# Squares of u on POOL and ACT only, sums of e on POOL only, with another order table

## The chip, the core and the metric

The kernel runs on one core of one Trainium2 chip. The metric is the device time of one execution in microseconds; lower is better. Before the change three runs gave 202.01, 202.43 and 203.88 us, median 202.43 us.

## What is computed

The reference does two steps. The first is attention without softmax over 8 batches of 8 heads, 576 tokens and 64 channels: per head `kv = k^T v`, `o = q kv`, and `o` is divided by its root mean square over the 64 channels and multiplied by `g_norm`. The second step takes the 4608 tokens of 512 channels through a feed-forward layer:

```python
h = x @ w_in                       # 512 -> 1024
e = np.exp(h - h_max)
solu = h * e / (sum(e) + 1e-9)
ln = (solu - mu) / np.sqrt(var + 1e-6) * g_ln
out = ln @ w_out                   # 1024 -> 512
```

The kernel never forms `solu`. It forms `u = h * exp(h)`, and for the layer norm it needs per token the sum of u, the sum of the squares of u, and the sum of e (only for the 1e-6 term). The mean is taken out of `w_out` beforehand, so the matmul `out = u @ w_out` needs only a factor per token at the end.

## The kernel before, in words

The 4608 tokens are cut into 9 chunks (`c` = 0 to 8) of 512. Chunks 0 to 7 hold the first 512 tokens of a batch, chunk 8 the 64 that are left of each. Each chunk passes through these pieces, whose names the texts below use:

- loads by the POOL queue: `k.c.g`, `v.c.g`, `q.c.g`, `q_last.c` (lines 298 and 308), and once `w_in`, `w_out`;
- `qT_mm`, `qT`: q is transposed on TensorE and copied out (chunks 0 to 3), or transposed by a DMA from the SP queue (chunks 4 to 8);
- `kv_mm`, `kv`: k^T v on TensorE, copied to `kvd` by DVE or ACT (line 210);
- `o_mm`, `sq`, `s_mm`, `ln`, `ex`, `x`: q kv on TensorE, squares on ACT, their mean over a head by a matmul, its -1/2 power in two ACT instructions, and the product on DVE;
- `h.c.f.part`: for each of 8 blocks f of 128 hidden channels, a matmul of x by w_in into a PSUM bank (line 464), in two halves for chunks 0 to 2;
- `exp.c.f` on ACT (line 471) and `u.c.f` on DVE (line 475): `e` in f32, `u` in bf16;
- `usq.c.f`: the square of u, bf16, 128x512 (line 479, by the helper `square` in lines 212 to 216; on ACT it is an activation, on POOL and DVE a tensor_tensor with u as both inputs);
- `es.c.n`: the sum of two neighbouring e, f32 to bf16 (lines 481 to 483), a tensor_tensor with two inputs in SBUF;
- `sums.c`: matmuls that sum u, usq and es over the hidden channels (line 508), so it needs all 8 u, 8 usq and 4 es of the chunk; then `turn.c`, `stats.c` (DVE) and `rstd.c` (ACT);
- `out.c.m.part` (line 562), `ob.c.m` (scaling by rstd on DVE or ACT) and `store.c.m`.

Nothing is scheduled at run time by hand: the pieces are issued in the order of the string `ORDER` (lines 20 to 88) by `Plan.emit`, and every engine carries out its own instructions in that order. A suffix such as `:dve` or `:act` names the engine; without one, it is the first in the piece's list of engines, as in

```python
add(("usq", c, f), "pool|act|dve", lambda e, c=c, f=f: u_sq(e, c, f), [("u", c, f)], [("u", c), ("usq", c)])
add(("es", c, n), "pool|dve", lambda e, c=c, n=n: e_sum(e, c, n), [("exp", c, f - 1), ("exp", c, f)], [("e", c, n), ("es", c)])
```

A buffer pool bounds how far pieces may run ahead: 3 buffers each for k, v, q and qT, 4 for e (each holds two blocks), 2 each for u, usq and es, 4 for ob. An `exp` that takes a fifth e buffer waits for the `es` and the two `u` that read the first one. The string `HOME` says in which kind of PSUM bank (h, out, o, s, misc; 8 banks in all) a piece's result lies where it is not the usual one.

Before the change the 72 squares are 32 on POOL, 29 on DVE and 11 on ACT; the 36 sums of e are 24 on POOL and 12 on DVE. POOL also issues the 36 loads.

Of the kernel before, what the change touches and what calls it, by code (L numbers as in the profile page):

```python
# [20 lines left out]
warm k.0.0 q.0.0 v.0.0 v.0.1 k.0.1 q.0.1 w_in.1 ident turn_g warm.0 qT_mm.0.0 warm.3 kv_mm.0.0 kv.0.0.2:act warm.1  # L21
kv.0.0.1:act qT.0.0 kv.0.0.0 o_mm.0.0 warm.4 warm.5 g_mean sq.0.0.1 sq.0.0.0 s_mm.0.0.0 s_mm.0.0.1 w_in.0 q.1.0 v.1.0
k.1.0 ex.0.0.1 q.1.1 kv_mm.0.1 kv.0.1.1 x.0.0.1 qT_mm.0.1 qT.0.1 kv.0.1.0:act k.1.1 kv.0.1.2:act warm.2 warm.6
ex.0.0.0 o_mm.0.1 sq.0.1.1 sq.0.1.0 x.0.0.0 s_mm.0.1.1 h.0.6.0 ex.0.1.1 s_mm.0.1.0 ex.0.1.0 x.0.1.1 h.0.4.0 h.0.7.0
x.0.1.0 h.0.3.0 table h.0.7.1 h.0.6.1 h.0.2.0 exp.0.7 h.0.4.1 qT_mm.1.0 h.0.3.1 v.1.1 exp.0.4 exp.0.6 h.0.2.1 u.0.7
qT.1.0 w_out.0 exp.0.3 h.0.1.0 w_out.1 h.0.0.0 u.0.6 exp.0.2 h.0.1.1 exp.0.1 u.0.3 kv_mm.1.0 kv.1.0.2:act kv.1.0.1:act
h.0.0.1 u.0.2 q.2.0 kv.1.0.0 u.0.4 h.0.5.0 usq.0.3:dve u.0.1 o_mm.1.0 exp.0.0 qT_mm.1.1 h.0.5.1 sq.1.0.1 qT.1.1
s_mm.1.0.1 k.2.0 usq.0.7 v.2.0 es.0.1 es.0.3 usq.0.6 sq.1.0.0 kv_mm.1.1 q.3.0 ln.1.0.1 u.0.0 usq.0.2:dve s_mm.1.0.0
exp.0.5 kv.1.1.2 kv.1.1.0 kv.1.1.1 o_mm.1.1 u.0.5 ex.1.0.1 ln.1.0.0 sq.1.1.0 w_mean.0 s_mm.1.1.0 ex.1.0.0 es.0.0
sq.1.1.1 ln.1.1.0 s_mm.1.1.1 ln.1.1.1 x.1.0.1 es.0.2:dve usq.0.0 usq.0.5 x.1.0.0 usq.0.4:dve ex.1.1.0 ex.1.1.1 x.1.1.0  # L30
usq.0.1 h.1.3.0 h.1.1.0 x.1.1.1 w_mean.1 sums.0 w_center.2 turn.0 h.1.5.0 w_center.0 v.4.0 h.1.1.1 qT_mm.2.0 h.1.2.0
exp.1.1 w_center.1 h.1.0.0 k.4.0 u.1.1 stats.0 h.1.3.1 h.1.0.1 qT.2.0:act k.3.0 w_center.3 w_center.5 v.3.0 out.0.0.0
qT_mm.2.1 exp.1.3 out.0.0.1 w_center.4 h.1.5.1 rstd.0 exp.1.0 qT.2.1:act w_center.6 w_center.7 u.1.3 u.1.0 h.1.2.1
out.0.0.2 exp.1.5 exp.1.2 kv_mm.2.0 h.1.4.0 out.0.0.3 kv.2.1.1:act kv.2.0.0 kv.2.0.2:act u.1.2 kv.2.1.0:act v.6.0
h.1.4.1 kv.2.0.1:act kv.2.1.2:act o_mm.2.0 qT_mm.3.0 ob.0.0 qT.3.0 es.1.0 q.4.0 sq.2.0.0 out.0.1.0 usq.1.3 sq.2.0.1
s_mm.2.0.0 out.0.1.1 qT.4 out.0.2.0 ln.2.0.0 exp.1.4 out.0.1.2 s_mm.2.0.1 out.0.1.3 ex.2.0.0 out.0.2.1 ln.2.0.1 u.1.5
u.1.4 ob.0.1:act ex.2.0.1 qT_mm.3.1 h.1.6.0 o_mm.2.1 sq.2.1.1 x.2.0.1 out.0.2.2 h.1.6.1 s_mm.2.1.1 out.0.3.0 qT.3.1
sq.2.1.0 exp.1.6 x.2.0.0 u.1.6 ln.2.1.1 usq.1.5 usq.1.1 out.0.2.3 s_mm.2.1.0 out.0.3.1 h.1.7.0 es.1.1 ln.2.1.0
ex.2.1.1 out.0.3.2 ex.2.1.0 x.2.1.1 ob.0.2 kv_mm.4.0 h.2.0.0 h.1.7.1 x.2.1.0 kv.4.1.0 usq.1.4:dve kv.4.1.1 out.0.3.3
exp.1.7 h.2.6.0 kv.4.0.0:act kv.4.0.1:act ob.0.3:act kv.4.0.2:act kv.4.1.2:act h.2.4.0 h.2.7.0 h.2.4.1 es.1.2:dve  # L40
usq.1.0 h.2.0.1 h.2.6.1 h.2.7.1 kv_mm.3.0 usq.1.6 store.0.0 store.0.1 u.1.7 usq.1.2:dve store.0.3 es.1.3 exp.2.4
exp.2.0 exp.2.7 u.2.4 h.2.2.0 h.2.5.0 h.2.3.0 h.2.5.1 usq.2.4 u.2.0 kv.3.0.2 store.0.2 kv.3.1.2:act exp.2.6 u.2.7
usq.1.7:dve kv.3.0.1:act h.2.1.0 kv.3.1.1 u.2.6 q_last.7 h.2.2.1 kv.3.0.0 exp.2.5 h.2.1.1 kv.3.1.0 exp.2.2 o_mm.3.0
exp.2.1 usq.2.0 es.2.3 sq.3.0.1 u.2.5 sums.1 s_mm.3.0.1 u.2.2 sq.3.0.0 turn.1 h.2.3.1 out.1.0.0 es.2.0 ln.3.0.1 u.2.1
exp.2.3 stats.1 usq.2.1:dve o_mm.3.1 out.1.0.1 u.2.3 s_mm.3.0.0 out.1.2.0 usq.2.2:dve rstd.1 sq.3.1.0 sq.3.1.1 ob.1.0
ex.3.0.1 x.3.0.1 usq.2.7 s_mm.3.1.1 out.1.2.1 ln.3.0.0 out.1.1.0 s_mm.3.1.0 ex.3.0.0 ln.3.1.1 q_last.2 ln.3.1.0
ex.3.1.0 es.2.2:dve x.3.0.0 out.1.1.1 ob.1.2 out.1.3.0 o_mm.4.1 ex.3.1.1 x.3.1.0 sq.4.1.0 out.1.3.1 x.3.1.1 sq.4.1.1
s_mm.4.1.0 usq.2.3:dve h.3.0.1 ln.4.1.0 ob.1.3 ex.4.1.0 ob.1.1 x.4.1.0 exp.3.0 h.3.7.1 v.5.0 h.3.3.1 k.5.0 usq.2.5
es.2.1 exp.3.7 usq.2.6:dve u.3.7 u.3.0 exp.3.3 s_mm.4.1.1 o_mm.4.0 sums.2 ln.4.1.1 sq.4.0.1 turn.2 ex.4.1.1 stats.2
h.3.2.1 store.1.0 sq.4.0.0 h.3.1.1 s_mm.4.0.1 exp.3.2 x.4.1.1 u.3.3 u.3.2 rstd.2 h.3.6.1 s_mm.4.0.0 ln.4.0.1 q_last.4  # L50
out.2.3.0 ex.4.0.1 q.5.0 k.6.0 h.3.5.1 x.4.0.1 qT.5 store.1.2 ln.4.0.0 exp.3.6 out.2.3.1 exp.3.5 exp.3.1 ex.4.0.0
u.3.6 kv_mm.5.0 kv_mm.6.0 ob.2.3 kv.5.0.0:act kv.5.1.2:act kv.5.1.0:act usq.3.3 x.4.0.0 u.3.5 kv.6.1.1 kv.5.1.1:act
es.3.1 h.3.4.1 kv.6.1.2:act store.1.1 k.7.0 kv.5.0.1:act out.2.1.0 exp.3.4 kv.5.0.2 o_mm.5.0 out.2.1.1 kv.6.0.2 u.3.4
sq.5.0.0 kv.6.1.0:act kv.6.0.1:act u.3.1 v.7.0 es.3.3 q_last.5 q_last.3 store.1.3 s_mm.5.0.0 ln.5.0.0 sq.5.0.1 ob.2.1
out.2.2.0 q.6.0 q_last.6 usq.3.5:dve o_mm.5.1 kv.6.0.0 out.2.2.1 ex.5.0.0 sq.5.1.1 sq.5.1.0 ob.2.2:act es.3.0
s_mm.5.0.1 store.2.3 out.2.0.0 qT.6 s_mm.5.1.1 usq.3.6 ln.5.1.1 out.2.0.1 x.5.0.0 ob.2.0 usq.3.7 ln.5.0.1 h.4.5.1
kv_mm.7.0 h.4.1.1 ex.5.1.1 ex.5.0.1 x.5.1.1 es.3.2 kv.7.1.2 usq.3.1:dve exp.4.5 usq.3.4:dve u.4.5 kv.7.1.0:act h.4.6.1
h.4.4.1 s_mm.5.1.0 usq.3.2 exp.4.1 exp.4.6 exp.4.4 ln.5.1.0 x.5.0.1 u.4.6 kv.7.0.2 usq.3.0 usq.4.5 kv.7.1.1 u.4.1
h.4.3.1 ex.5.1.0 x.5.1.0 exp.4.3 h.4.0.1 sums.3 h.4.2.1 h.4.7.1 usq.4.1:dve u.4.4 kv.7.0.0:act store.2.2 exp.4.0 u.4.0
turn.3 exp.4.2 u.4.3 stats.3 u.4.2 exp.4.7 h.5.0.1 out.3.1.0 o_mm.6.0 out.3.1.1 out.3.3.0 rstd.3 kv.7.0.1 u.4.7  # L60
usq.4.2:dve sq.6.0.0 s_mm.6.0.0 ob.3.1:act out.3.3.1 store.2.0 out.3.0.0 ln.6.0.0 store.2.1 ob.3.3:act sq.6.0.1
out.3.2.0 es.4.0 usq.4.3:dve usq.4.0:act ex.6.0.0 s_mm.6.0.1 out.3.0.1 q_last.1 store.3.1 es.4.1 out.3.2.1 usq.4.7
x.6.0.0 usq.4.6:dve usq.4.4:dve es.4.2 ob.3.0:act ln.6.0.1 es.4.3 exp.5.0 q.7.0 ex.6.0.1 u.5.0 qT.7 o_mm.6.1 h.5.1.1
sums.4 h.5.3.1 ob.3.2 sq.6.1.0 sq.6.1.1 exp.5.1 exp.5.3 turn.4 s_mm.6.1.0 h.5.2.1 x.6.0.1 h.5.6.1 ln.6.1.0 store.3.3
exp.5.2 ex.6.1.0 exp.5.6 u.5.1 stats.4 u.5.3 h.5.5.1 out.4.1.0 s_mm.6.1.1 ln.6.1.1 u.5.2 u.5.6 exp.5.5 x.6.1.0
out.4.1.1 u.5.5 h.5.4.1 out.4.3.0 rstd.4 h.5.7.1 ex.6.1.1 x.6.1.1 ob.4.1 exp.5.7 exp.5.4 out.4.0.0 u.5.7 es.5.1
usq.5.0 q_last.0 o_mm.7.0 u.5.4 out.4.3.1 store.3.2 ob.4.3 out.4.0.1 sq.7.0.1 store.3.0 usq.5.5:dve sq.7.0.0
s_mm.7.0.1 s_mm.7.0.0 es.5.3:dve ob.4.0 usq.5.1 usq.5.7:act es.5.2 es.5.0:dve ln.7.0.0 out.4.2.0 h.6.7.1 ex.7.0.0
h.6.2.1 usq.5.3:dve x.7.0.0 out.4.2.1 ln.7.0.1 usq.5.6:dve h.6.4.1 qT.8 h.6.1.1 store.4.1 exp.6.7 usq.5.4:act usq.5.2
exp.6.2 ob.4.2 ex.7.0.1 u.6.2 exp.6.1 u.6.7 store.4.0 x.7.0.1 sums.5 o_mm.7.1 turn.5 exp.6.4 sq.7.1.0 sq.7.1.1 h.6.6.1  # L70
stats.5 h.6.0.1 s_mm.7.1.0 u.6.1 u.6.4 exp.6.6 store.4.2 u.6.6 s_mm.7.1.1 h.6.5.1 exp.6.0 h.6.3.1 out.5.1.0 u.6.0
usq.6.4:dve ln.7.1.0 ln.7.1.1 exp.6.5 exp.6.3 out.5.2.0 u.6.5 es.6.3 store.4.3 out.5.0.0 out.5.1.1 usq.6.0 usq.6.2:act
ex.7.1.0 ex.7.1.1 u.6.3 x.7.1.0 out.5.2.1 x.7.1.1 rstd.5 o_mm.8.0 out.5.0.1 out.5.3.0 sq.8.0.1 sq.8.0.0 ob.5.2
s_mm.8.0.0 out.5.3.1 ob.5.1:act store.5.1 ln.8.0.0 es.6.1 s_mm.8.0.1 ob.5.0 usq.6.5:dve h.7.6.1 es.6.2:dve store.5.0
ob.5.3 store.5.3 usq.6.7:dve h.7.7.1 es.6.0:dve h.7.3.1 usq.6.1 ln.8.0.1 usq.6.3 ex.8.0.0 exp.7.7 exp.7.3 exp.7.6
x.8.0.0 usq.6.6:dve u.7.7 es.7.3:dve h.7.2.1 store.5.2 exp.7.2 out.6.3.0 u.7.3 sums.6 h.7.5.1 out.6.3.1 turn.6
ex.8.0.1 x.8.0.1 exp.7.5 out.6.2.0 u.7.2 stats.6 u.7.5 u.7.6 o_mm.8.1 out.6.2.1 sq.8.1.0 sq.8.1.1 rstd.6 s_mm.8.1.0
ob.6.3:act out.6.0.0 s_mm.8.1.1 ln.8.1.0 usq.7.2 ln.8.1.1 ex.8.1.1 out.6.0.1 h.7.1.1 exp.7.1 ob.6.2 ex.8.1.0 u.7.1
# [78 lines left out]
def kernel(  # L157
# [35 lines left out]
    add = plan.add  # L193
# [36 lines left out]
    q_last = big.tile([128, NP, B, D], BF16, name="q_last")  # L230
# [254 lines left out]
    for c in range(NC):  # L485
        for f in range(NF):
# [9 lines left out]
            if f % 2:  # L496
                n = f // 2
                add(("es", c, n), "pool|dve", lambda e, c=c, n=n: e_sum(e, c, n), [("exp", c, f - 1), ("exp", c, f)], [("e", c, n), ("es", c)])
# [135 lines left out]
```

## Time and profile before

| | |
|---|---|
| median of three runs | 202.43 us (202.01 to 203.88) |
| profiled execution, its own time | 204.0 us |
| its span, first to last instruction | 202.2 us |
| mean granted TensorE clock | 0.975 |
| PE busy | 178.0 us, 88% |
| DVE busy | 142.1 us, 70% |
| ACT busy | 141.2 us, 70% |
| POOL busy | 96.5 us, 48% |
| DMA | 29.71 MB, mean 147 GB/s |

Engines are PE (TensorE matmul), DVE (VectorE), ACT (ScalarE), POOL (GpSimd) and SP (a queue that issues DMAs). The profile page gives busy time per engine, forty equal slices of the span with the busy share of each in tenths, the groups of instructions with their mean duration, and the chain of work that ended last. The trace gives the same by window, by tile and as a timeline; there a row has start, duration, engine, line and shape, and in brackets the idle time of the engine in front of it with what ended it. Consecutive matmuls overlap at their ends, so the distance from start to start is the cost of one in a run, and the same holds to a lesser degree for ACT and DVE.

### The profile page before, as it was taken

The page shows a single profiled execution, that of the slowest core. Times are in us where ns is not written, and L with a number is a line of the kernel's source. Part 1 is how long each engine was busy: PE and PEld are TensorE (multiplying, and loading weights), DVE is VectorE, ACT ScalarE, POOL GpSimd, SP SyncE. Part 2 cuts the span into 40 slices and gives each one's busy share as a digit, 9 for nine tenths or more (in the row PEclk, how much of TensorE's full clock was granted, in tenths as well). Part 3 has the DMA queues.
Part 4 walks back from the last instruction along what each step waited for, and adds up shares of the span by engine and source line. Part 5 has one row for each costly group of instructions (what it writes and reads, how often), then busy time and mean ns, then how long its engine had stood idle before and what let it go on. Part 6 is the DMA issues. An engine that isn't in the chain of part 4 may idle for free.

```text
span 202.2 us, 5289 instructions
## 1 busy us (share of the span) xinstructions
PE 178.0 (88%) x2174; PEld 87.0 (43%) x2199; DVE 142.1 (70%) x266; ACT 141.2 (70%) x250; POOL 96.5 (48%) x106
## 2 busy tenths in 40 slices
PE   7677955999999488999869999999999999989991
PEld 2342532564444143355224544544544454445540
DVE  1145699688489988877847973869986782799440
ACT  2068873567989496998947769969796749885232
POOL 7942894805934994029961383164065031506000
PEclk9999996699999999999978999999999999999999
DMA  3999999999988769999997327787510622230265
GB/s 54 194 204 207 206 385 229 207 208 208 209 135 186 143 65 188 225 212 172 212 156 181 85 16 119 143 170 156 130 28 3 149 63 70 59 79 3 69 148 203
DMA packets 35544, 29.71 MB, mean 147 GB/s; under 512 B 16440, under 2 KB 30016, under 8 KB 35520
## 3 DMA queue, kind: packets, MB, share of 16 engines
q0 software_dynamic: 19104, 17.30, 52.1%
q1 hardware_dynamic: 16128, 11.54, 24.5%
q10 hardware_dynamic: 288, 0.52, 0.7%
q8 instruction: 17, 0.28, 0.6%
q14 instruction: 7, 0.06, 0.1%
HBM read 32.51 MB, written 9.44 MB: 207 GB/s over the span
## 4 chain that ended last, share of the span: by engine, by line
PE 53%; DVE 20%; ACT 14%; issue 5%; DMA 5%; POOL 1%; ACTq 0%; DVEq 0%; POOLq 0%
PE out_ps L562 21%; PE h_ps L464 19%; DVE u_sb L475 6%; PE misc_ps L508 5%; DVE usq_sb L216 5%; ACT e_sb L471 4%; DMA v_sb<-in_v_dram 3%; PE s_ps L407 3%; ACT osq_sb L214 3%; ACT rst_sb L415 3%; ACT lss_sb L411 2%; PE o_ps L395 2%; DVE x_sb L427 2%; DVE kvd L210 2%; DMA out_dram<-ob_sb 2%
## 5 line engine op out<-in xcount | busy, mean ns | idle before, releaser
L562 PE MATMUL out_ps<-w_out_sb,u_sb 128*128 128x512 bf16 x279 | 70.4, 384 | 2.3 <-DVE u_sb L475 1.4
L464 PE MATMUL h_ps<-x_sb,w_in_sb 128*128 128x512 bf16 x274 | 69.2, 384 | 2.0 <-issue 0.7
L471 ACT ACTIVATE e_sb<-h_ps,zero_t 128x512 f32<-128x512 f32 x72 | 47.6, 686 | 14.3 <-PE h_ps L464 13.1
L475 DVE TENSOR_TENSOR u_sb<-h_ps,e_sb 128x512 bf16<-128x512 f32 x72 | 47.6, 683 | 10.8 <-ACT e_sb L471 10.2
L216 POOL TENSOR_TENSOR usq_sb<-u_sb 128x512 bf16<-128x512 bf16 x32 | 34.2, 1078 | 41.5 <-DVE u_sb L475 12.7
L483 POOL TENSOR_TENSOR es_sb<-e_sb 128x512 bf16<-128x512 f32 x24 | 31.0, 1294 | 31.0 <-ACT e_sb L471 31.0
L562 PEld LDWEIGHTS <-u_sb 128*128 128x128 bf16 x288 | 27.4, 98 | 34.7 <-issue 4.2
L464 PEld LDWEIGHTS <-w_in_sb 128*128 128x128 bf16 x288 | 27.1, 99 | 34.2 <-issue 4.8
L427 DVE SCALAR_TENSOR_TENSOR x_sb<-o_ps,g_rep,rst_sb 128x512 bf16<-128x512 f32 x36 | 26.3, 742 | 13.5 <-ACT rst_sb L415 11.5
L214 ACT ACTIVATE osq_sb<-o_ps,zero_t 128x512 bf16<-128x512 f32 x36 | 23.2, 684 | 9.7 <-PE o_ps L395 9.5
L411 ACT ACTIVATE lss_sb<-s_ps,eps_t 128x512 f32<-128x512 f32 x32 | 21.3, 684 | 10.5 <-PE s_ps L407 10.4
L216 DVE TENSOR_TENSOR usq_sb<-u_sb 128x512 bf16<-128x512 bf16 x29 | 25.3, 881 | 0.0
L222 DVE TENSOR_SCALAR ob_sb<-out_ps,rstd 128x512 f32<-128x512 f32 x23 | 17.0, 745 | 9.6 <-PE out_ps L562 5.1
L415 ACT ACTIVATE rst_sb<-lss_sb,zero_t 128x512 f32<-128x512 f32 x32 | 22.5, 722 | 0.2
L407 PE MATMUL s_ps<-osq_sb,head_mean 128*128 128x512 bf16 x36 | 13.8, 401 | 6.8 <-DVE qT_sb L210 3.3
L395 PE MATMUL o_ps<-qT_sb,kvd 64*64 64x256 bf16 (+1 forms) x192 | 9.1, 259 | 5.0 <-DVE kvd L210 4.4
L298 POOL DMA_DIRECT2D v_sb<-in_v_dram x10 | 7.5, 754 | 8.9 <-PE s_ps L343 8.3
L220 ACT ACTIVATE ob_sb<-out_ps,rstd 128x512 f32<-128x512 f32 (+1 forms) x14 | 9.1, 657 | 3.8 <-PE out_ps L562 3.1
L508 PEld LDWEIGHTS <-stat_sel 128*32 128x32 bf16 x720 | 10.1, 97 | 3.2 <-issue 3.1
L210 ACT CAST kvd<-misc_ps 64x128 bf16<-64x128 f32 (+1 forms) x16 | 4.2, 260 | 9.4 <-PE misc_ps L343 8.1
L483 DVE TENSOR_TENSOR es_sb<-e_sb 128x512 bf16<-128x512 f32 x12 | 10.1, 847 | 0.7 <-ACT e_sb L471 0.7
L210 DVE COPY qT_sb<-misc_ps 128x1024 bf16<-128x1024 bf16 x6 | 4.1, 685 | 7.9 <-PE misc_ps L376 7.9
(57 smaller groups left out, 136.8 us busy)
## 6 DMA issues: line engine op xcount, KB each, us to landing
out_dram<-ob_sb SPq DMA_DIRECT2D x66, 128.0 KB, 2.4
k_sb<-in_k_dram POOLq DMA_DIRECT2D x6, 576.0 KB, 11.8
v_sb<-in_v_dram POOLq DMA_DIRECT2D x6, 576.0 KB, 10.1
q_sb<-in_q_dram POOLq DMA_DIRECT2D x6, 512.0 KB, 10.2
w_out_f<-in_moe_w_out_dram POOLq DMA_DIRECT2D x2, 1024.0 KB, 13.9
k_sb<-in_k_dram POOLq DMA_DIRECT2D x4, 288.0 KB, 10.6
v_sb<-in_v_dram POOLq DMA_DIRECT2D x4, 288.0 KB, 10.0
q_sb<-in_q_dram POOLq DMA_DIRECT2D x4, 256.0 KB, 10.3
```

The lines of the kernel that those rows point to most:

```text
L214: nc.scalar.activation(out=dst, in_=src, func=AF.Square, bias=zero_t[:, :])
L216: on[engine].tensor_tensor(out=dst, in0=src, in1=src, op=MUL)
L407: nc.tensor.matmul(t[:, :], head_mean[:, :], T["osq", i][:, :], start=True, stop=True)
L411: nc.scalar.activation(out=t[:, :], in_=T["s", i][:, :], func=AF.Ln, bias=eps_t[:, :])
L415: nc.scalar.activation(out=t.rearrange("p a b c -> p (a b c)"), in_=T["lss", i][:, :], func=AF.Exp, scale=-0.5, bias=zero_t[:, :])
L427: nc.vector.scalar_tensor_tensor(out=t[:, 2 * hf:2 * hf + 2, z], in0=T["o", c, hf, z][:, :, :, :], scalar=g_rep[:, :], in1=T["rst", (c, hf ...
L464: nc.tensor.matmul(bank(("h", c, f), [128, 512])[:, :], w_in_sb[:, dt, f * 128:(f + 1) * 128], T["x", c][:, dt].rearrange("p a b c -> p (a ...
L471: nc.scalar.activation(out=t[:, f % 2, :], in_=T["h", c, f][:, :], func=AF.Exp, bias=zero_t[:, :])
L475: nc.vector.tensor_tensor(out=t[:, f, :], in0=T["h", c, f][:, :], in1=T["e", c, f // 2][:, f % 2, :], op=MUL)
L483: on[engine].tensor_tensor(out=t[:, n, :], in0=e[:, 0, :], in1=e[:, 1, :], op=ADD)
L508: nc.tensor.matmul(t[32 * j:32 * j + 32, 0, :], stat_sel[:, i, :], cols, start=(part == 0 and n == 0), stop=(part == 2 and n == n_src - 1) ...
L562: nc.tensor.matmul(bank(("out", c, m), [128, d_model])[:, :], T["u", c][:, f, m * 128:(m + 1) * 128], w_out_sb[:, f, :], start=(f == 0), s ...
```

## The change

Two lines lose DVE from their list of engines, and both strings, `ORDER` and `HOME`, are replaced as a whole.

```diff
-            add(("usq", c, f), "pool|act|dve", lambda e, c=c, f=f: u_sq(e, c, f), [("u", c, f)], [("u", c), ("usq", c)])
+            add(("usq", c, f), "pool|act", lambda e, c=c, f=f: u_sq(e, c, f), [("u", c, f)], [("u", c), ("usq", c)])
...
-                add(("es", c, n), "pool|dve", lambda e, c=c, n=n: e_sum(e, c, n), [("exp", c, f - 1), ("exp", c, f)], [("e", c, n), ("es", c)])
+                add(("es", c, n), "pool", lambda e, c=c, n=n: e_sum(e, c, n), [("exp", c, f - 1), ("exp", c, f)], [("e", c, n), ("es", c)])
```

In the new order 52 squares are on POOL, 20 on ACT and none on DVE, and all 36 sums are on POOL. Of the other pieces that may go to two engines, DVE and ACT share the copies of kv 26 to 22 (21 to 27 before) and the scalings ob 21 to 16 (23 to 14 before). The pieces themselves, their number, shapes and buffers are the same. The passage in which the first squares, sums and loads of chunk 2 stand, before:

```
h.0.0.1 u.0.2 q.2.0 kv.1.0.0 u.0.4 h.0.5.0 usq.0.3:dve u.0.1 o_mm.1.0 exp.0.0 qT_mm.1.1 h.0.5.1 sq.1.0.1 qT.1.1
s_mm.1.0.1 k.2.0 usq.0.7 v.2.0 es.0.1 es.0.3 usq.0.6 sq.1.0.0 kv_mm.1.1 q.3.0 ln.1.0.1 u.0.0 usq.0.2:dve s_mm.1.0.0
```

and after:

```
h.0.5.0 w_out.0 h.0.0.0 h.0.5.1 h.0.4.1 table w_out.1 exp.0.5 exp.0.4 h.0.6.1 h.0.1.0 es.0.2 h.0.0.1 exp.0.6 exp.0.0
...
usq.0.6 h.0.7.1 ln.1.0.0 s_mm.1.0.1 kv_mm.1.1 exp.0.7 q.2.0 ln.1.0.1 kv.1.1.2:act kv.1.1.0 kv.1.1.1 ex.1.0.0 o_mm.1.1
sq.1.1.1 usq.0.0 usq.0.2 k.2.0 es.0.0 x.1.0.0 ex.1.0.1 s_mm.1.1.1 sq.1.1.0 x.1.0.1 es.0.1 v.2.0 u.0.7 w_mean.0
```

and its end, after:

```
out.7.0.1 ob.7.0 turn.8 out.8.1.0 store.7.2 out.8.2.1 store.7.3 store.7.0 stats.8 out.8.0.1 out.8.3.0 out.8.1.1 rstd.8
out.8.3.1 ob.8.2:act ob.8.0 ob.8.1:act store.8.0 store.8.2 store.8.1 ob.8.3.1:act ob.8.3.0 store.8.3.0:act store.8.3.1
```

## The prediction

> **What bounds the kernel now.** I read the page's busy times and slices first, then the costliest groups, then the timelines of DVE, POOL and PE beside each other.
>
> ```profile
> span 202.2 us, 5289 instructions
> ...
> PE 178.0 (88%) x2174; PEld 87.0 (43%) x2199; DVE 142.1 (70%) x266; ACT 141.2 (70%) x250; POOL 96.5 (48%) x106
> ...
> PEclk9999996699999999999978999999999999999999
> ```
>
> PE is the bound, but it has two passages at a lower clock, around slices 7 and 21. By windows PE is busy 85.8 of the first 104.0 us and 92.2 of the last 98.2 us: what can be won lies in the first half. The groups of the change:
>
> ```profile
> L216 POOL TENSOR_TENSOR usq_sb<-u_sb 128x512 bf16<-128x512 bf16 x32 | 34.2, 1078 | 41.5 <-DVE u_sb L475 12.7
> L483 POOL TENSOR_TENSOR es_sb<-e_sb 128x512 bf16<-128x512 f32 x24 | 31.0, 1294 | 31.0 <-ACT e_sb L471 31.0
> ...
> L216 DVE TENSOR_TENSOR usq_sb<-u_sb 128x512 bf16<-128x512 bf16 x29 | 25.3, 881 | 0.0
> ```
>
> The mean of DVE's squares hides two kinds. The tile view of `usq_sb` has their spread (least, median, greatest):
>
> ```profile
> L216 DVE TENSOR_TENSOR usq_sb<-u_sb x29: 392/415/3923, 26.4 to 187.0; 128x512 bf16<-128x512 bf16 x29
> ```
>
> A square costs DVE 0.41 us, or several. The timeline of DVE shows the four long ones and one victim, that of POOL what ran beside the first:
>
> ```profile
> 26.35 3.92 DVE L216 TENSOR_TENSOR usq_sb<-u_sb 128x512 bf16<-128x512 bf16 x1
> ...
> 30.80 0.68 DVE L210 COPY qT_sb<-misc_ps 128x1024 bf16<-128x1024 bf16 x1
> ...
> 66.18 2.90 DVE L216 TENSOR_TENSOR usq_sb<-u_sb 128x512 bf16<-128x512 bf16 x1
> ...
> 73.48 2.54 DVE L216 TENSOR_TENSOR usq_sb<-u_sb 128x512 bf16<-128x512 bf16 x1
> ...
> 99.14 3.60 DVE L216 TENSOR_TENSOR usq_sb<-u_sb 128x512 bf16<-128x512 bf16 x1
> ```
>
> ```profile
> 24.44 2.51 POOL L483 TENSOR_TENSOR es_sb<-e_sb 128x512 bf16<-128x512 f32 x2
> 26.91 1.03 POOL L216 TENSOR_TENSOR usq_sb<-u_sb 128x512 bf16<-128x512 bf16 x1
> 27.89 0.81 POOL L298 DMA_DIRECT2D q_sb<-in_q_dram  x1
> 28.71 1.27 POOL L483 TENSOR_TENSOR es_sb<-e_sb 128x512 bf16<-128x512 f32 x1
> ```
>
> POOL worked without a break from 24.44 to 29.98; DVE's square ended at 30.27. The one at 99.14 ended at 102.74, POOL's run of sums and squares at 102.44; the one at 73.48 at 76.02, POOL's sum at 75.73. So a DVE instruction that reads two operands from SBUF stands still while POOL computes, and everything behind it on DVE stands too. The other DVE groups take one operand from PSUM and show nothing of this (u 683 ns, 0.60 from start to start). On PE it arrives as:
>
> ```profile
> 31.54 0.39 PE L407 MATMUL s_ps<-osq_sb,head_mean 128*128 128x512 bf16 x1 [3.34 <-DVE qT_sb L210]
> 33.06 0.96 PE L395 MATMUL o_ps<-qT_sb,kvd 64*64 64x256 bf16 x8 [1.14 <-DVE kvd L210]
> ...
> 70.38 0.50 PE L395 MATMUL o_ps<-qT_sb,kvd 64*64 64x256 bf16 x8 [2.60 <-DVE kvd L210]
> ...
> 102.99 0.39 PE L407 MATMUL s_ps<-osq_sb,head_mean 128*128 128x512 bf16 x1 [2.32 <-DVE kvd L210]
> ```
>
> A fourth wait, 1.42 us in front of 76.68, is for a u behind the square at 73.48.
>
> **Part 1, removed: DVE's squares and sums.** Idle time of PE: 3.34 + 1.14 + 2.60 + 1.42 + 2.32 = 10.8 us. After the first and the last, PE also ran at half clock (windows: 0.50 from 34 to 38 us). There four matmuls of line 545 took 2.08 us against 1.09 later, two of line 407 0.88 against 0.43, single ones of line 464 about 0.43 against 0.22: 2.3 us in all. From 103 to 108 us, groups of four matmuls took 1.11, 1.71 and 1.25 us against 0.86, and one of line 407 0.43 against 0.22: 1.7 us. Together **14.8 us** that hang on four blocked squares. In the second half DVE's squares (at most 1.26 us) hold nobody up, since POOL is busy 30.5 of 98.2 us there; taking them away gains nothing.
>
> **Part 2, added to ACT.** 9 squares more at 0.717 us are 6.5 us, 2 scalings more and 5 kv copies fewer cancel (2 x 0.69 - 5 x 0.26 = 0.1). ACT goes from 141 to 148 of some 190 us. Between two `sums` its work by start-to-start costs is 12 to 20 us against 12 to 24 of PE: hidden. I take 0; if a square stood in front of an awaited `sq` or `exp` each time, 9 x 0.7 = 6.3 us.
>
> **Part 3, added to POOL.** 20 squares of 1.04 and 12 sums of 1.27 us are 36 us: 96.5 becomes 133. What matters is whether POOL delivers before `sums.c` asks. I added up along the new order, with 1.02 us per square, 1.25 per sum, 0.77 per load, and for PE 0.216 per matmul of 512 columns and 1.23 per `sums`. From sums.1 to sums.2 POOL has 13.5 us in 17.1 of PE, to sums.3 14.2 in 15.1, to sums.4 16.5 in 23.6, after that 10 to 12 in 12 to 19. The tightest place is chunk 2: from es.2.0 to usq.2.0 POOL has 4 sums, 5 squares and 9 loads, 17.0 us, and es.2.0 can start 0.8 us after a matmul that lies 18.4 us of PE before sums.2. Left: **0.6 us**. At the other sums 2.3 to 7.6 us are left. POOL's late sums also hold e buffers: exp.1.5 waits for es.0.3, which by the same addition is ready **2.3 us** after h.1.5. ACT then stands, with PE's banks behind it. I charge 2.3 us.
>
> The Trainium skill, "GPSIMD Engine Reference", section 4.1 "Engine selection", speaks against parts 1 and 3: elementwise work belongs on VectorE, as GpSimd takes about twice as long with two inputs. The trace agrees on single instructions: 1.04 against 0.41 us, 1.27 against 0.68. By that rule alone 20 x 0.63 + 12 x 0.59 = 20 us are added. "SBUF — State Buffer", section "SBUF: two separate sides", names the other side: a DVE instruction with two SBUF inputs and a GpSimd one that reads SBUF exclude each other for the whole instruction. The 3.92 us here agree, and by it the blocked time vanishes. The trace decides for the second, as POOL is off PE's path and DVE was on it.
>
> **Part 4, moved loads.** POOL's queue now has es.0.2, usq.0.6, usq.0.0, usq.0.2, es.0.0 and es.0.1 ahead of v.2.0, and those wait for ACT and DVE. Following them step by step, v.2.0 is issued at about 32.6 us; before, at 23.6. It landed 17.6 us later, at 41.2, since DMA moved 205 to 208 GB/s without a break until 52 us, and the 8.06 MB up to v.2.0 need 39.3 us at 205 plus 2 at the start. The same bytes lie ahead of it now, and when it is issued two earlier loads are still under way, so it should land at 41 to 42 us again. PE comes to kv_mm.2.0 after 33.7 us of own work, plus 5.4 lost at the start (as before) and 1.8 in the chain sq, s_mm, ln of chunk 1: 40.9. I charge **1.0 us**; ends: 0, if other stalls cover it, and 9.2, if it lands 17.6 us after issue as in its own row. Later loads come out 3 us or more ahead of use. Stores and transposes of SP keep their places within a few us of PE work, with 82.8 us of waiting in SP before: 0.
>
> **Part 5, the end.** Behind sums.8, PE had 5.1 us of work and 4.6 us followed. Now PE has 6.0 (out.7.0.1 is moved behind it), and ob.7.0 stands in front of turn.8 on DVE. The chain 0.86 + 0.75 + 0.33 + 0.45 + 0.6 gives rstd 3.2 us after sums.8, within PE's 6.0, then 0.5 for the last half scaling and 3.4 for a store. The wait of ACT's last scaling for a store, 0.60 us, goes. Sum **+0.3 us**.
>
> **Part 6, the rest of the table.** The order of every engine differs. The blocked squares also covered what else would be late at 28 to 40 us: 1.0 us. No row shows the new order's other waits. PE's own work adds up to 175.8 us, so the span lost 26.4: 5.4 at the start, 14.8 above, 4.6 at the end, 1.6 elsewhere. Ends are thus -1.6 and, by the stretch at 66 to 78 us as the nearest row of a new wait, +4.0; I take 0.
>
> **Sum:** -14.8 + 2.3 + 1.0 + 0.3 + 1.0 = -10.2 us: span 192.0, this execution's time 204.0 - 10.2 = 193.8. It lay 1.6 us above the median, and part of that may be blocked time that varies from run to run. From the median, 202.43 - 10.2 = 192.2. I take the middle, **193.0 us**.
>
> **Rivals.**
> - *The gain is half eaten by POOL*: its 37% more work makes sums.2, sums.4 and the e buffers late by 1 to 2 us each, and one gap halves the clock again (2 us). 193.0 + 5.5 = 198.5. For: 0.6 us left. Against: POOL is idle 50 us in the second half. Chance 0.16.
> - *The change doesn't do what it says*: ACT or PE's banks hold up the same matmuls as soon as DVE doesn't, and the 14.8 us remain as other waits: 202.4. Against: from 104 us on PE runs nearly without gaps under the same banks. Chance 0.08.
> - *Slower, by the loads*: POOL issues v.2.0 9 us late and it lands 9 us late, because DMA runs dry. kv_mm.2.0 waits 9.2 instead of 1.0 us, the half clock returns (2.3), and q.3.0, issued behind two squares and two sums more (4.5 us), is late by 2: 193.0 + 8.2 + 2.3 + 2 = 205.5. It decides from a landing past 50 us. Chance 0.14.
>
> The forecast, 188 to 197.5 us, has 0.62. The low end is the median less all 14.8 us, 187.6; to leave out no more than 2 in 10 the range must take in the half-eaten case: 188 to 201. This kernel's runs spread by about 1%, so within 1% counts as no change. Faster 0.62 + 0.16 = 0.78, same 0.08, slower 0.14.
>
> **What would show it.** Right: DVE busy near 107 us with no instruction over 1.3 us; no PE gap over 2 us after 30 us; clock 9 in all slices after the start; POOL near 133 us. Wrong: PE waiting for POOL at line 505 (the `sums` line now), a wait of ACT exp for es above 3 us, kv_mm.2.0 behind a DMA past 43 us, or POOL's instructions longer than 1.04 and 1.27 us.

## The result, and the profile after

The change makes the kernel faster: median 194.86 us (194.12 to 197.04, four runs) against 202.22 us (201.58 to 203.88); ratio **0.961, 95% interval 0.953 to 0.970**. The profiled execution took 194.12 us, its span is 192.3 us. The profiled execution before was a slow one (204.0 us at a mean clock of 0.975), the one after was not (0.982), so the two traces lie 9.9 us apart and the medians 7.4. The page of the kernel after, busy times, granted clock and the two groups of the change on POOL (all line numbers are 3 lower than before):

```profile
span 192.3 us, 5320 instructions
...
PE 179.1 (93%) x2199; PEld 88.1 (46%) x2199; DVE 110.8 (58%) x228; ACT 146.3 (76%) x256; POOL 129.6 (67%) x138
...
PEclk9879998899999999999999999999999999999999
...
L213 POOL TENSOR_TENSOR usq_sb<-u_sb 128x512 bf16<-128x512 bf16 x52 | 53.4, 1040 | 21.3 <-DVE u_sb L472 21.2
...
L480 POOL TENSOR_TENSOR es_sb<-e_sb 128x512 bf16<-128x512 f32 x36 | 45.4, 1275 | 20.2 <-issue 11.9
```

By these two traces PE does the same work in 9.9 us less. DVE lost 31.3 us of busy time, POOL gained 33.1. POOL's squares now take 1040 ns on average where it was 1078, and the tile view says that none is stretched any more (least, median, greatest):

```profile
L213 POOL TENSOR_TENSOR usq_sb<-u_sb x52: 1028/1039/1082, 23.7 to 174.0; 128x512 bf16<-128x512 bf16 x52
```

The waits of 3.34, 2.60 and 2.32 us are gone from PE's timeline. Its gaps behind the start, up to 60 us:

```profile
30.50 0.73 PE L392 MATMUL o_ps<-qT_sb,kvd 64*64 64x256 bf16 x8 [1.01 <-DVE kvd L207]
32.01 0.58 PE L404 MATMUL s_ps<-osq_sb,head_mean 128*128 128x512 bf16 x1 [0.78 <-ACT osq_sb L211]
49.53 0.24 PE L505 MATMUL misc_ps<-usq_sb,stat_sel 128*32 128x128 bf16 x4 [1.57 <-issue]
```

After that PE is never idle for more than 0.55 us until the end. What remains is the short chain of chunk 1, and a wait of 1.57 us within sums.0 for which the profile shows no cause.

### The profile page after: what moved, and what is told of

It is laid out like the page before. It is cut to its first block, busy times and chain, and to the rows that moved or that the text cites. A ratio compares the mean times of both kernels' runs of the same rounds, so it can differ in the third digit from the quotient of the medians.

```text
span 192.3 us, 5320 instructions
## 1 busy us (share of the span) xinstructions
PE 179.1 (93%) x2199; PEld 88.1 (46%) x2199; DVE 110.8 (58%) x228; ACT 146.3 (76%) x256; POOL 129.6 (67%) x138
## 4 chain that ended last, share of the span: by engine, by line
PE 70%; DMA 9%; POOL 6%; ACT 5%; DVE 4%; issue 4%; POOLq 0%; ACTq 0%
PE h_ps L461 26%; PE out_ps L559 25%; DMA k_sb<-in_k_dram 9%; PE misc_ps L505 5%; PE o_ps L392 3%; PE s_ps L404 3%; ACT osq_sb L211 2%; PE misc_ps L340 2%; PE misc_ps L373 2%; POOL v_sb L295 2%; DVE x_sb L424 2%; PE out_ps L542 1%; PE s_ps L275 1%; POOL k_sb L295 1%; ACT e_sb L468 1%
## 5 line engine op out<-in xcount | busy, mean ns | idle before, releaser
L461 PE MATMUL h_ps<-x_sb,w_in_sb 128*128 128x512 bf16 x288 | 70.4, 381 | 0.1
L559 PE MATMUL out_ps<-w_out_sb,u_sb 128*128 128x512 bf16 x288 | 68.9, 379 | 0.1
L213 POOL TENSOR_TENSOR usq_sb<-u_sb 128x512 bf16<-128x512 bf16 x52 | 53.4, 1040 | 21.3 <-DVE u_sb L472 21.2
L480 POOL TENSOR_TENSOR es_sb<-e_sb 128x512 bf16<-128x512 f32 x36 | 45.4, 1275 | 20.2 <-issue 11.9
L219 DVE TENSOR_SCALAR ob_sb<-out_ps,rstd 128x512 f32<-128x512 f32 (+1 forms) x21 | 15.3, 734 | 14.0 <-PE out_ps L559 11.0
L211 ACT ACTIVATE usq_sb<-u_sb,zero_t 128x512 bf16<-128x512 bf16 x20 | 13.8, 715 | 1.0 <-DVE u_sb L472 1.0
L217 ACT ACTIVATE ob_sb<-out_ps,rstd 128x512 f32<-128x512 f32 (+1 forms) x16 | 10.5, 672 | 2.5 <-PE out_ps L559 2.0
L207 DVE CAST kvd<-misc_ps 64x128 bf16<-64x128 f32 (+1 forms) x17 | 4.9, 288 | 11.3 <-ACT kvd L207 11.0
L275 PE MATMUL s_ps<-zeros 128*128 128x512 bf16 x26 | 9.3, 495 | 1.2 <-DVE zeros L238 1.2
L340 PEld LDWEIGHTS <-k_sb 64*64 64x64 bf16 x576 | 7.1, 110 | 4.7 <-issue 3.8
```

The costliest lines, as they stand in the source:

```text
L211: nc.scalar.activation(out=dst, in_=src, func=AF.Square, bias=zero_t[:, :])
L213: on[engine].tensor_tensor(out=dst, in0=src, in1=src, op=MUL)
L461: nc.tensor.matmul(bank(("h", c, f), [128, 512])[:, :], w_in_sb[:, dt, f * 128:(f + 1) * 128], T["x", c][:, dt].rearrange("p a b c -> p (a ...
L480: on[engine].tensor_tensor(out=t[:, n, :], in0=e[:, 0, :], in1=e[:, 1, :], op=ADD)
L559: nc.tensor.matmul(bank(("out", c, m), [128, d_model])[:, :], T["u", c][:, f, m * 128:(m + 1) * 128], w_out_sb[:, f, :], start=(f == 0), s ...
```

## The experiments

Theory: a DVE instruction that works from SBUF to SBUF stands still while POOL computes, and PE waited behind four of these. Rivals: the new order table makes the gain, whatever the engines; or the long DVE squares have another cause. Eight kernels were run.

**Only the four longest squares leave DVE, in the old table.**

```diff
-usq.0.3:dve ... usq.1.7:dve ... usq.2.1:dve ... usq.3.5:dve
+usq.0.3:act ... usq.1.7:act ... usq.2.1:act ... usq.3.5:act
```

> The kernel before with its own order table; only the four squares that stood longest on DVE (usq.0.3, usq.1.7, usq.2.1, usq.3.5: 3.92, 2.90, 2.54, 3.60 us) go to ACT, at the same places. Theory (the gain comes from DVE no longer standing still while POOL computes): the waits of PE behind them (3.34 + 1.14, 2.60 + 1.42, 2.32 us) and the half clock after two of them (4.0 us) go; other DVE squares remain and may be blocked in turn, so some 8 to 13 of 202.2 us go: 189 to 194.5 us. Rival (the gain comes from the new order table, the blocked squares only stand where PE would wait anyway): 200 us or more.

Measured: 196.55 us, ratio 0.972 (0.963 to 0.981). Four words of the table bring 2.8% of 3.9, so most of the gain doesn't need the new table. It is less than forecast (189 to 194.5), for two reasons that the trace shows: the next DVE square stands in the place of the first, and at the place of the fourth most of the wait stays. DVE and PE of this kernel:

```profile
28.23 2.10 DVE L216 TENSOR_TENSOR usq_sb<-u_sb 128x512 bf16<-128x512 bf16 x1
...
94.82 0.75 DVE L222 TENSOR_SCALAR ob_sb<-out_ps,rstd 128x512 f32<-128x512 f32 x1 [2.69 <-PE out_ps L562]
```

```profile
30.98 0.73 PE L395 MATMUL o_ps<-qT_sb,kvd 64*64 64x256 bf16 x8 [2.04 <-DVE kvd L210]
...
95.83 0.39 PE L407 MATMUL s_ps<-osq_sb,head_mean 128*128 128x512 bf16 x1 [1.59 <-DVE kvd L210]
```

The square is usq.0.2, 0.41 us before when it came after the block. The second wait was 2.32 us before; 1.59 are left although no square stands there: DVE itself is idle for 2.69 us, until it can do a scaling that lies ahead of the kvd copy.

**The engines of the change without its table.** All 29 DVE squares go to ACT and all 12 DVE sums to POOL, at their old places.

```diff
-usq.c.f:dve   (29)      -es.c.n:dve   (12)
+usq.c.f:act             +es.c.n
```

> The kernel before with its own order table, all 29 DVE squares on ACT and all 12 DVE sums on POOL, at the same places: the change without its table. Theory: the 14.8 us of blocked time and half clock go, but this table was not made for it. ACT gets 29 x 0.72 = 21 us more (141 to 162 us busy), POOL 15 us. sums.0 had nothing left on POOL and gets 1.3 us later. Expected 190 to 197 us. Rival (the table makes the gain): 200 us or more, as ACT's 21 us land in front of awaited instructions.

Measured: 198.67 us, ratio 0.983 (0.976 to 0.991): slower than the four words alone, and outside the forecast (190 to 197), though not as slow as the rival had it (200 or more). Nothing stands on DVE any more (110.9 us busy), but ACT is at 156.5 us, and PE waits in many small places: 0.79 and 0.56 us for `sq`, 1.67 for a v load, 1.08 for a scaling on ACT. So the engines alone bring 1.7%. That the work added to ACT and POOL makes the rest of the loss fits these waits, but no run separates it.

**POOL's reading made short.** Order and engines as before; POOL computes 8 of 512 columns of its squares and sums and writes a constant into the others, so that part of the sums is left out.

```diff
+        elif engine == "pool":
+            nc.gpsimd.tensor_tensor(out=dst[:, 0:8], in0=src[:, 0:8], in1=src[:, 0:8], op=MUL)
+            nc.gpsimd.memset(dst[:, 8:512], 4096.0)
```

> The kernel before, order and engines unchanged, but POOL computes only 8 of the 512 columns of each of its squares and sums and fills the others with a constant (a part of the computation is left out). POOL's instructions that read SBUF become short. Theory (DVE's instruction with two SBUF inputs stands while POOL's reads SBUF): all 29 DVE squares take about 0.41 us, the sums about 0.68, no PE gap over 1.5 us after 25 us, and the time is 186 to 192 us. Rival (DVE's long squares have another cause, such as the load on SBUF from DMA or PE): several squares still take over 2 us and the time stays above 198 us.

Measured: 193.61 us, ratio 0.961 (0.950 to 0.972). The tile views of usq and es in this kernel:

```profile
L216 POOL TENSOR_TENSOR usq_sb<-u_sb x32: 188/199/618, 22.9 to 171.8; 128x8 bf16<-128x8 bf16 x32
L217 POOL MEMSET usq_sb<- x32: 507/518/556, 23.0 to 172.0; 128x504 bf16 x32
L219 DVE TENSOR_TENSOR usq_sb<-u_sb x29: 399/415/435, 26.3 to 174.7; 128x512 bf16<-128x512 bf16 x29
```

```profile
L490 DVE TENSOR_TENSOR es_sb<-e_sb x12: 677/682/694, 31.1 to 173.8; 128x512 bf16<-128x512 f32 x12
```

DVE's instructions are untouched, and not one of the 29 squares takes over 0.435 us, where the longest was 3.92; no sum over 0.694, where the longest was 1.52. POOL's fills of 0.52 us, which write SBUF but read nothing, don't stretch them. That settles the cause: POOL's instructions that read SBUF. It isn't the load from DMA, which from 20 to 60 us moved as much as before (287, 228, 208 and 188 GB/s in steps of 10 us against 291, 224, 208 and 183). Nor does the gain come from POOL being done sooner (68.9 us busy against 96.5): in the kernel before the profile shows no engine waiting for its squares or sums. The time lies 1.6 us over the forecast (186 to 192), and one PE gap of 1.68 us, for a q transpose, is over the 1.5 us that were allowed.

**DVE's share put back into the new table.** The 29 squares and 12 sums that DVE had are on DVE again, at their new places.

```diff
-usq.c.f, usq.c.f:act   es.c.n      (29 and 12 of the new table)
+usq.c.f:dve            es.c.n:dve
```

> The kernel after the change with its new table, but the 29 squares and 12 sums that the kernel before had on DVE are on DVE again, at their new places. POOL gets lighter, DVE has room (58% busy in the new kernel). Theory: wherever POOL works without a break the DVE instruction stands, several take over 2 us, and PE waits behind them: 197 to 206 us. Rival (the new table makes the gain; the engines matter little): 193 to 196 us.

Measured: 199.36 us, ratio 0.984 (0.973 to 0.995), 4.5 us over the kernel after. The tile view and two of PE's new waits:

```profile
L213 DVE TENSOR_TENSOR usq_sb<-u_sb x29: 399/416/1480, 31.5 to 184.2; 128x512 bf16<-128x512 bf16 x29
```

```profile
64.04 1.46 PE L461 MATMUL h_ps<-x_sb,w_in_sb 128*128 128x512 bf16 x6 [1.40 <-DVE u_sb L472]
...
95.47 0.41 PE L392 MATMUL o_ps<-qT_sb,kvd 64*64 64x256 bf16 x8 [1.32 <-DVE ob_sb L219]
```

The time is as forecast, the sight is not: no square over 2 us, although POOL is as busy as before the change (98 us). Where the squares fall beside POOL's work differs, and with it how long they stand. Three waits of PE for DVE are new, of 1.40, 1.32 and 1.10 us. They aren't all blocked time; in front of the first DVE has

```profile
62.09 1.29 DVE L213 TENSOR_TENSOR usq_sb<-u_sb 128x512 bf16<-128x512 bf16 x2
```

where two undisturbed squares take 0.75 us. So this run doesn't say how much of the 4.5 us is standing still and how much is plain work ahead of an awaited u. The new table alone brings 1.6%, the engines alone 1.7%, both 3.9%; with the intervals given, 3.9 can't be told from their sum.

**One input in place of two.** Old table and engines; DVE's squares become u times 2, with one operand from SBUF. The squares of these blocks are left out.

```diff
+        elif engine == "dve":
+            nc.vector.tensor_scalar_mul(out=dst, in0=src, scalar1=2.0)
```

> The kernel before, order and engines unchanged, but DVE's 29 squares are replaced by u times 2 (tensor_scalar, one input in SBUF instead of two; the squares of these blocks are left out of the sums). If only two SBUF inputs on DVE stand against POOL: all 29 under 0.5 us, DVE's 12 sums still up to 1.5 us, time 192 to 196 us. If the one-input form also needs the port that POOL holds: several of 2 to 4 us again, time 200 to 203 us.

Measured: 200.61 us, ratio 0.993 (0.988 to 0.997). Its tile view and DVE's timeline:

```profile
L216 DVE TENSOR_SCALAR usq_sb<-u_sb x29: 267/284/3460, 26.9 to 184.3; 128x512 bf16<-128x512 bf16 x29
```

```profile
29.06 2.38 DVE L216 TENSOR_SCALAR usq_sb<-u_sb 128x512 bf16<-128x512 bf16 x1
64.18 2.76 DVE L216 TENSOR_SCALAR usq_sb<-u_sb 128x512 bf16<-128x512 bf16 x1
71.34 2.40 DVE L216 TENSOR_SCALAR usq_sb<-u_sb 128x512 bf16<-128x512 bf16 x1
96.86 3.46 DVE L216 TENSOR_SCALAR usq_sb<-u_sb 128x512 bf16<-128x512 bf16 x1
```

Undisturbed it needs 0.28 us, less than the square's 0.41, and it stands just the same; the time is in the range forecast for that case (200 to 203). So my reading that it takes two operands from SBUF was too narrow. The Trainium skill, "SBUF — State Buffer", section "SBUF: two separate sides", names this second kind as well: a DVE instruction in a mode that uses both ports. The trace doesn't show modes; it shows the stall.

**All squares on POOL.** In the new table ACT's 20 squares go to POOL.

```diff
-usq.c.f:act   (20)
+usq.c.f
```

> The kernel after the change, with the 20 squares that ACT has moved to POOL at the same places: POOL 129.6 + 20 x 1.04 = 150 us, ACT 146 - 14 = 132 us. Theory of the additions along the order (0.6 us left in front of sums.2, 3.6 in front of sums.8): chunk 2 gets 2 squares, 1.5 us late; chunk 8 gets 6 squares, 2.5 us late; the e buffers are freed later at the start (3 squares of chunk 0, up to 3 us). 3 to 7 us slower than the kernel after: 198 to 202 us. Rival (POOL has room, as it is idle for a third of the span): within 1 us of the kernel after, 194 to 196 us.

Measured: 205.30 us, slower than before: ratio 1.017 (1.009 to 1.026), some 10 us over the kernel after, more than forecast. PE's timeline at sums.2 and sums.8, then the clock:

```profile
84.03 0.63 PE L505 MATMUL misc_ps<-usq_sb,stat_sel 128*32 128x128 bf16 x32 [1.41 <-POOL usq_sb L213]
...
188.45 0.29 PE L505 MATMUL misc_ps<-usq_sb,stat_sel 128*32 128x128 bf16 x8 [2.62 <-POOL usq_sb L213]
189.45 0.30 PE L505 MATMUL misc_ps<-usq_sb,stat_sel 128*32 128x128 bf16 x4 [0.70 <-POOL usq_sb L213]
190.44 0.62 PE L505 MATMUL misc_ps<-usq_sb,stat_sel 128*32 128x128 bf16 x16 [0.70 <-POOL usq_sb L213]
```

```profile
PEclk9789996999999999999999999999999999999578
```

sums.2 waits 1.4 us where 1.5 were forecast, sums.8 4.0 where 2.5 were, and the clock falls behind that wait (0.50 over 190 to 195 us), which I had left out: the last 28 out matmuls take 8.35 us where they took 6.22. A further wait of 1.77 us at 94.12 us has no cause in the profile. POOL idle for a quarter of the span is no reserve where its work is due.

**Only the sums back on DVE**, and **ACT's squares moved to DVE**, both in the new table:

```diff
-es.c.n       (12)          -usq.c.f:act   (20)
+es.c.n:dve                 +usq.c.f:dve
```

> The kernel after the change, with only the 12 sums that the kernel before had on DVE back on DVE; squares as after. It splits the 4.5 us that 29 squares and 12 sums on DVE cost together. If every DVE instruction with two SBUF inputs costs its own blocked time: 12 sums of 0.68 to 1.5 us, in all 8 us more on DVE with 2 us of it blocked: 195 to 197 us. If the squares alone make the loss: 194 to 195 us.

> The kernel after the change, with its 20 ACT squares moved to DVE at the same places; POOL keeps its 52 squares and 36 sums. ACT gets 14 us lighter, DVE (58% busy) 8 us heavier if nothing stands. Theory: POOL is denser here than in the kernel before, so several of the 20 stand for 1 to 4 us and PE waits behind some: 196 to 202 us. Rival (engine load decides, DVE is the quickest at a square): 192.5 to 195 us.

Measured: 197.43 us, ratio 0.978 (0.971 to 0.985), and 197.83 us, ratio 0.979 (0.972 to 0.987): 2.6 and 3.0 us over the kernel after. The tile views of es in the first and of usq in the second:

```profile
L480 DVE TENSOR_TENSOR es_sb<-e_sb x12: 679/764/2189, 21.7 to 180.8; 128x512 bf16<-128x512 f32 x12
```

```profile
L213 DVE TENSOR_TENSOR usq_sb<-u_sb x20: 409/532/2789, 36.8 to 183.6; 128x512 bf16<-128x512 bf16 x20
```

The sums stand too: 12.5 us in all against 12 x 0.68 = 8.2. But the time is 0.4 us over the forecast (195 to 197), and that blocked sums cost it isn't shown: PE waits 2.16 us for a k load at 90.75 us (0.55 in the kernel after), for a reason not followed up, with a clock of 0.83 from 90 to 100 us, and for DVE no longer than in the kernel after (1.00 us). In the other, ACT is 12.4 us lighter and DVE only at 63%, PE waits 1.58, 1.39 and 1.02 us for DVE, and it is slower all the same, as forecast (196 to 202); the rival by engine load falls.

## Why the prediction was right, point by point

Forecast 193.0 us, range 188 to 201; measured 194.86.

- **Part 1, the blocked squares.** The mechanism is shown: POOL's short reads free all 41 DVE instructions, and four words alone bring 2.8%. The size was too large. Compared at the start of the `sums`, the kernel with POOL's reads short gains 5.2 us up to sums.0 (34.57 against 39.79), 3.0 more to sums.1, 0.1 to sums.2 and 2.7 to sums.3: 11.0 where the sum had 14.8; by the ratio and by the medians it gains 7.9 and 9.0 us in all. The gaps were added up as if nothing else were late behind them, and something was: 0.90 us for a kvd copy at 29.55, 0.32 for a u, 1.68 for a q transpose at 90.08 in that kernel. With the four squares on ACT, 1.59 of the 2.32 us stay. Nor is the half clock behind such a stall a fixed price: from 30 to 40 us the kernel before has 0.66, the one-input kernel, with the same table and a wait of 3.06 us at 32.10, 0.83, which is 0.17 x 10 = 1.7 us less by estimate. One reading of the lines was wrong, that the long squares end with POOL's run of work; see the last section.
- **Part 2, ACT: 0.** Holds in the new table (146.3 us; the longest PE wait for ACT is 0.79). In the old one, with 29 more squares on ACT, PE waits up to 1.08 us for it (second experiment).
- **Part 3, POOL.** The tightest place was found: usq.2.0, the last square of chunk 2, ends at 81.77 us, and the part of sums.2 that reads the squares starts at 82.38: 0.6 us left, as forecast. With two squares more there PE waits 1.41. The 2.3 us charged for exp.1.5 behind es.0.3 were too much: ACT waited for POOL 0.75 us at 38.81, one exp before exp.1.5, and PE had no gap between 33 and 47 us, having matmuls of other blocks to do. (POOL issues 42 loads, not the 36 named above.)
- **Part 4, loads.** v.2.0 was issued at 33.16 us (32.6 forecast) and landed 7.7 us later, at 40.9 (41 to 42 forecast):

```profile
33.16 0.78 POOL L295 DMA_DIRECT2D v_sb<-in_v_dram  x1
```

```profile
v_sb<-in_v_dram POOLq DMA_DIRECT2D x1, 576.0 KB, 7.7
```

  PE came to kv_mm.2.0 at 43.9. So 0, not 1.0 us. Issued 9.5 us later, it landed at the same time: the 16 DMA engines were at least 90% busy from 5 to 50 us in both. The sum behind the 41 us had two slips: the loads up to v.2.0 are 8064 KB of 1024 bytes, 8.26 MB and not 8.06, and before the change DMA did not move 205 to 208 GB/s throughout, as two slices between 25 and 36 us have 385 and 229. The rival that ended on the slower side needed a landing past 50.
- **Part 5, the end.** 10.0 us from the end of sums.8 (182.3) to the end, 9.7 before: +0.3 as forecast. But 0.9 us of it is matmul work that was moved there from ahead of sums.8 and should not have been charged; behind the last matmul 3.9 us are left where it was 4.5.
- **Part 6.** 1.0 us was charged at 28 to 40 us; two gaps (1.8 us) and a lower clock (0.83 over 30 to 40 us, so 0.17 x 10 = 1.7 us) are there, and with them one of the signs of being right fails, the clock of 9 in all slices. The 1.57 us within sums.0 was in no part.
- **The sum** gave 193.8 us for a profiled execution, and that one took 194.12. That they lie so close is luck. Of the 26.4 us that the span before had over PE's own work (175.8 us by the prediction's addition), the forecast left 16.2, and 16.5 are there, but in other places: 3.3 charged for POOL and the load in parts 3 and 4 cost nothing; 28 to 40 us costs 3.5 in place of 1.0; the start about 5.8 in place of 5.4, of which 1.7 is a lower clock (0.91 and 0.92 over the first 20 us); gaps elsewhere 2.9 in place of 1.6, most of it in sums.0; the end 3.9 in place of 4.9. Most of the 1.9 us of error was made in the last step, from the execution to the median. I took the 1.6 us by which the execution before lay over its median for blocked time in part, and went halfway down; the execution after lies 0.7 us *under* its median.

## What to carry to other kernels

Ask for the least, the median and the greatest duration of a group, not for its mean: 0.41 and 3.92 us stand behind 881 ns. An engine can be idle half of the time, as POOL before the change, and still be what stops another. Here work from SBUF to SBUF was better off on an engine that POOL doesn't block (ACT's squares take 0.705 to 0.749 us throughout in the kernel after). If it goes to POOL itself, add up POOL's work in front of the due times, not over the span. When work moves between engines, the order counts as much: engines alone and table alone brought 1.7 and 1.6%, together 3.9%, and four words at the right places 2.8%.

## What was not expected of the hardware

- A blocked DVE instruction can wait for more than one POOL instruction: before the change, at 26.35 us, it stood through the rest of a sum, a square, the issue of a DMA and another sum. So the 3.92 us agree with the two excluding each other, but not for a single instruction of POOL (a sum takes 1.45 us at most). It need not wait until POOL has nothing left, though. The square at 66.18 us ended at 69.08 and the one at 99.14 at 102.74, each within a run of POOL that goes on:

```profile
67.52 2.68 POOL L483 TENSOR_TENSOR es_sb<-e_sb 128x512 bf16<-128x512 f32 x2
...
102.38 2.24 POOL L216 TENSOR_TENSOR usq_sb<-u_sb 128x512 bf16<-128x512 bf16 x2
```

  These pairs are 0.2 us longer than undisturbed ones (2.51 and 2.06). So the prediction's reading that POOL's run ended at 102.44 is wrong; at which POOL instruction a blocked one gets its turn is left open. POOL's own stretching is far smaller (a square of 1.49 us at most against 1.04).
- The clock fell to 0.83 over 30 to 40 us in the kernel after behind gaps of no more than 1.01 and 0.78 us, while before it had stayed at 1.00 behind a gap of 2.60 us at 70 us, and with only the sums back on DVE it stayed at 1.00 over 30 to 40 us behind the same two gaps (1.00 and 0.78). What decides it is left open.
- The wait within sums.0, with no releaser in the profile, is there in every kernel with the new table (1.05 to 1.83 us) and in none with the old. DMA is saturated there, and in the kernel after one packet of DMA queue q14, kind instruction, lies in that time. But with DVE's share put back, and with ACT's squares on DVE, the wait is there without such a packet, so that PE waited for its instructions isn't shown; the cause stays open.
